# Six leading transfers reordered, and the early step order of five engines written out as a list, in a fused attention and channel-mix kernel

## The chip, the cores and the metric

The kernel runs on one core of a Trainium2 chip. The metric is the device time of one execution in microseconds; the number given for a kernel is the median of its runs. Five engines matter here, each of which executes its own instructions strictly in the order of the program: TensorE (PE, matmul; PEld is its weight load), VectorE (DVE), ScalarE (ACT), GpSimd (POOL) and SyncE (SP), which in this kernel issues every transfer between HBM and on-chip memory.

## What is computed

The reference, cut to what matters (B, H, S, D = 8, 8, 576, 64; the channel mix has d_model 512 and d_ff 1024):

```python
def _attn_ref(q, k, v):
    k_p = k.reshape(B, H, S // 8, 8, D).mean(axis=3)      # 72 pooled keys per head
    v_p = v.reshape(B, H, S // 8, 8, D).mean(axis=3)
    scores = np.matmul(q, k_p.transpose(0, 1, 3, 2)) / np.sqrt(D)
    scores = scores - np.max(scores, axis=-1, keepdims=True)
    attn = np.exp(scores)
    attn = attn / (np.sum(attn, axis=-1, keepdims=True) + 1e-09)
    return np.matmul(attn, v_p)

def _moe_ref(x, mu_k, mu_r, w_k, w_v, w_r):               # x: attention, heads joined
    x_prev = x shifted by one token, zeros in front
    xk = mu_k * x + (1.0 - mu_k) * x_prev
    xr = mu_r * x + (1.0 - mu_r) * x_prev
    k = np.maximum(xk @ w_k, 0.0)
    v = k * k @ w_v
    r = 1.0 / (1.0 + np.exp(-(xr @ w_r)))
    return r * v
```

## The kernel before, in words

The 8 x 576 = 4608 tokens are cut into 13 chunks of 128, 256 and then eleven times 384 tokens, and each chunk into tiles of 128 tokens (36 tiles). A tile goes through `softmax` (scores on PE, maxima and sums on DVE, exponentials on ACT, norming on POOL or DVE) and `transposed`/`transposed_rest`; a chunk goes through `attended` (attention times pooled values, then the token shift and mix on ACT, POOL and DVE), `hidden` (x times w_k, squared ReLU), `gate` (x times w_r, sigmoid) and `mixed` (hidden times w_v, times the gate, and the store). The first two chunks multiply whole float32 operands; the later ones use three matmuls on operands split into a high and a low part. The three weights arrive as 64-bit words and are turned into float32 by `convert` (ACT and DVE) and into the two parts by `split` (ACT, then DVE or POOL).

Every transfer has a short name in the string `LOADS` (line 48): `k0`, `k1` are the keys of the first batch entry, heads 0 to 3 and 4 to 7 (576 KB each); `v0`, `v1` its values; `r0`, `r1` the values behind the last 8 pooled keys of batch entries 0 and 1, in a packed form of 128 KB each; `c0` the constants (54 KB: the mix factors `mu`, a mask and a selection matrix `pick`); `q0`, `q1` and so on the queries of one tile (256 KB each); `wk0`, `wr0`, `wv0` and so on a 512 KB slice of a weight. SP issues them in the order of the string, one behind the other. In the profile `k0` is `stage<-in_kT`, `k1` is `early_sl<-in_kT`, `r1` is `early_sl<-in_vp`, `r0` is `packed<-in_vp`, `c0` is `given<-in_consts`, `q0` is the first `qs<-in_qT`.

The first work on them, by step name:

- `keys 0 0` adds the 8 neighbours of `k0` by matmuls with the identity on PE (line 570, two halves of four sums), and ACT copies the sums to `kbd` (line 612).
- `keys 0 1` does the same for `k1` in three steps on DVE (line 559 twice, line 601 for `kbd`).
- `last_values 1` and `last_values 0` take `r1` and `r0`: a PE sum with `pick` from `c0` (line 659), a cast on ACT (line 668), a subtraction on DVE (line 670), and a spread by the mask (line 680 on DVE for `r1`, line 675 on ACT for `r0`).
- `complements` computes 1 - mu from `c0` on DVE (line 440).
- `softmax 0` and `part 0 1 2` are the two halves of tile 0: scores on PE at line 729, the maximum on DVE at line 753.
- `warm` (line 424) and `filling` (line 434) are matmuls on zeros and on the identity whose results nobody reads: 4 and 40 of them.

The program is written by a planner, the class `Order`. Every piece of work is a generator whose steps are named after it (`keys 0 1`, `hidden 2 4`) and yield an engine and an estimated length. The planner keeps a clock of its own for each engine, and picks, step by step, among the steps that could start first, the one with the earliest due time (`add` sets it; the table `EARLIER` shifts it). The order of its picks is the order of the instructions on each engine. A buffer that a step takes is the one that came free first by the planner's clock. If the string `PLAN` holds names, the planner takes those steps, in that order, before it chooses any itself, and while names are left the extra delay `spare` of a PE step is not added:

```python
at = max(self.free[eng],
    t[4][1] if t[4][0] == eng else t[1] + (t[5] if eng == "pe" and not self.plan else 0.0))
...
if self.plan:
    name = self.plan.pop(0)
    at, t = next((at, t) for at, t in ready if t[6] == name)
else:
    first = min(at for at, _ in ready)
    ...
```

In the kernel before, `PLAN` is empty: the planner chooses all 2821 steps.

Of the kernel before, what the change touches and what calls it, by code (L numbers as in the profile page):

```python
# [45 lines left out]
REBASE = 2.0 ** -((1023 - 127) // 8)  # L46

LOADS = (
    "k0 c0 r1 k1 r0 q0 wk0 q1 q2 v0 wk1 v1 wk2 q4 wk3 k2 wk4 q3 wk5 wk6 k3 wk7 wr0 wr1 wr2 wr3 v3 "
    "wv2 wv0 wv1 wv3 q5 wv4 wv5 wv6 v2 wv7 "  # L50
)

# [55 lines left out]
}  # L108
PLAN = ""
SPARE = 0.5  # L110
SECOND = 0.0
NEXT = 14.0
# [5 lines left out]
class Order:  # L118
# [8 lines left out]
    def __init__(self):  # L127
# [8 lines left out]
        self.plan = []  # L136
        for step in PLAN.split(", ") if PLAN else ():
            name, _, times = step.partition(" x")
# [1085 lines left out]
```

## Time and profile before

| | |
|---|---|
| median of 3 runs | 631.24 us (631.03 to 631.31) |
| the profiled execution | 631.48 us, of which 629.7 us lie between its first and its last instruction (the span) |
| instructions | 9238 |
| busy, share of the span | PE 99%, PEld 87%, DVE 63%, ACT 56%, POOL 34% |
| read and written in HBM | 40.43 MB and 9.44 MB |
| granted TensorE clock | 1.000 |

The busy times are sums of the durations that the profiler recorded; a PE that is busy may still be busy with matmuls that nobody needs (`warm` and `filling`). All transfers go through one queue (q1). The profiled execution took 0.24 us longer than the median; 1.8 us of it lie around the span.

### The profile page before, as it was taken

How to read it: one execution, taken by the hardware profiler on the slowest of the kernel's cores; microseconds unless marked ns; L12 is line 12 of the kernel's file. 1: busy time of each engine (PE TensorE's matmuls, PEld its weight loads, DVE VectorE, ACT ScalarE, POOL GpSimd, SP SyncE). 2: the span in 40 equal slices, each digit the busy share in tenths (PEclk: the TensorE clock that was granted, in tenths of full speed). 3: DMA queues.
4: the chain of work that ended last, by engine and by line, in shares of the span. 5: the costliest groups of instructions: out<-in, count | busy, mean ns of one | idle time of the engine just before them, and what ended most of it. 6: DMA issues, size and time to landing. Idle time of an engine off the chain costs nothing.

```text
span 629.7 us, 9238 instructions
## 1 busy us (share of the span) xinstructions
PE 622.3 (99%) x3355; PEld 548.0 (87%) x3355; DVE 394.2 (63%) x792; ACT 350.9 (56%) x755; POOL 215.3 (34%) x338
## 2 busy tenths in 40 slices
PE   8999999999999999999999999999999999999997
PEld 8986559988989989989988988988988988988986
DVE  5999969968824645937635665759854655553411
ACT  3776866766525855556645555545655556454320
POOL 1422287448015128128125019217415106104000
PEclk9999999999999999999999999999999999999999
DMA  8696332051330012411011051032100100000001
GB/s 309 233 364 217 108 128 89 18 179 52 125 110 34 0 34 82 137 34 51 0 34 52 25 193 45 6 137 78 55 34 34 33 18 35 17 1 18 33 1 50
DMA packets 19005, 50.45 MB, mean 80 GB/s; under 512 B 2256, under 2 KB 2512, under 8 KB 18960
## 3 DMA queue, kind: packets, MB, share of 16 engines
q1 hardware_dynamic: 18960, 49.87, 22.6%
q8 instruction: 26, 0.43, 0.3%
q14 instruction: 19, 0.16, 0.1%
HBM read 40.43 MB, written 9.44 MB: 79 GB/s over the span
## 4 chain that ended last, share of the span: by engine, by line
PE 88%; ACT 3%; DVE 3%; POOL 3%; DMA 2%; issue 1%; SPq 0%; POOLq 0%; ACTq 0%; DVEq 0%
PE mm L1029 30%; PE mm L1111 29%; PE mm L1078 16%; PE bank L931 5%; PE sc L729 4%; PE bank L833 2%; DMA got_wr<-in_w_r 1%; DMA stage<-in_kT 1%; PE bank L424 1%; PE bank L434 1%; PE bank L888 1%; POOL stage L559 1%; ACT e L776 0%; ACT tmp L522 0%; DVE got_wk L527 0%
## 5 line engine op out<-in xcount | busy, mean ns | idle before, releaser
L1029 PE MATMUL mm<-xkh,w_k 128*128 128x384 f32 x704 | 180.9, 337 | 0.0
L1111 PE MATMUL mm<-w_v,sh 128*128 128x512 f32 x528 | 173.3, 394 | 0.0
L1029 PEld LDWEIGHTS mm<-xkh,w_k 128*128 128x128 f32 x704 | 126.0, 188 | 1.0 <-issue 0.6
L1029 PE MATMUL mm<-xkl,w_k 128*128 128x384 f32 x352 | 117.7, 335 | 0.0
L1111 PEld LDWEIGHTS mm<-w_v,sh 128*128 128x128 f32 x528 | 99.3, 188 | 19.4
L1111 PE MATMUL mm<-w_v,sl 128*128 128x512 f32 x264 | 103.0, 390 | 0.0
L791 POOL TENSOR_TENSOR px<-e,sm 128x64 f32<-128x64 f32 (+1 forms) x33 | 10.9, 331 | 225.7 <-DVE sm L785 219.9
L1078 PE MATMUL mm<-w_r,xrh 128*128 128x512 f32 x264 | 86.0, 397 | 0.0
L985 DVE SCALAR_TENSOR_TENSOR xm<-bank,given,t 128x384 f32<-128x384 f32 x88 | 50.6, 612 | 40.2 <-POOL t L959 23.0
L944 ACT ACTIVATE t<-bank,om_sb 128x384 f32<-128x384 f32 (+1 forms) x96 | 47.9, 573 | 50.0 <-PE bank L931 49.8
L1052 ACT CAST sh<-rk 128x384 fp32r<-128x384 f32 x88 | 45.0, 513 | 50.2 <-DVE rk L1046 50.0
L1121 DVE TENSOR_TENSOR rs<-mm,rs 128x512 f32<-128x512 f32 x36 | 24.8, 689 | 70.9 <-PE mm L1111 70.7
L1054 DVE TENSOR_TENSOR sl<-rk,sh 128x384 fp32r<-128x384 f32 x88 | 51.9, 592 | 24.8 <-ACT sh L1052 24.4
L1029 PEld LDWEIGHTS mm<-xkl,w_k 128*128 128x128 f32 x352 | 66.1, 188 | 0.0
L1046 DVE SCALAR_TENSOR_TENSOR rk<-mm,rk 128x384 f32<-128x384 f32 x88 | 48.6, 553 | 17.4 <-ACT rk L1039 17.0
L1078 PEld LDWEIGHTS mm<-w_r,xrh 128*128 128x128 f32 x264 | 49.6, 188 | 10.2
L1003 POOL TENSOR_TENSOR xkl<-xm,xkh 128x384 fp32r<-128x384 f32 x44 | 44.7, 1017 | 37.2 <-ACT xkh L1001 37.1
L1111 PEld LDWEIGHTS mm<-w_v,sl 128*128 128x128 f32 x264 | 49.7, 188 | 8.7
L559 POOL TENSOR_TENSOR stage<-stage 128x512 f32<-128x512 f32 (+7 forms) x59 | 51.3, 878 | 13.7 <-DVE w_k L552 11.4
L1039 ACT ACTIVATE rk<-mm 128x384 f32<-128x384 f32 x88 | 43.0, 489 | 20.9 <-PE mm L1029 19.9
L1078 PE MATMUL mm<-w_r,xrl 128*128 128x512 f32 x132 | 51.4, 389 | 0.0
L1003 POOL TENSOR_TENSOR xrl<-xm,xrh 128x384 fp32r<-128x384 f32 x44 | 44.8, 1019 | 1.3 <-ACT xrh L1001 1.2
(144 smaller groups left out, 972.8 us busy)
## 6 DMA issues: line engine op xcount, KB each, us to landing
qs<-in_qT SPq DMA_DIRECT2D x36, 256.0 KB, 3.5
out<-rs SPq DMA_DIRECT2D x36, 256.0 KB, 2.0
stage<-in_kT SPq DMA_DIRECT2D x15, 576.0 KB, 3.8
stage<-in_vm SPq DMA_DIRECT2D x15, 512.0 KB, 4.5
got_wk<-in_w_k SPq DMA_DIRECT2D x8, 512.0 KB, 6.8
got_wv<-in_w_v SPq DMA_DIRECT2D x8, 512.0 KB, 7.5
stage<-in_vr SPq DMA_DIRECT2D x6, 384.0 KB, 4.1
got_wr<-in_w_r SPq DMA_DIRECT2D x4, 512.0 KB, 8.0
```

The lines of the kernel that those rows point to most:

```text
L559: nc_eng.tensor_tensor(out=st[:, :, :w], in0=st[:, :, :w], in1=st[:, :, w:2 * w], op=ALU.add)
L931: nc.tensor.matmul(out=xp[:, o], lhsT=v, rhs=p, start=(q == 0), stop=(q == len(terms) - 1))
L944: nc.scalar.activation(out=ts[m][:, 1:n + 1], in_=xp, func=AF.Copy, scale=om_sb[:, m, g:g + 1])
L985: nc.vector.scalar_tensor_tensor(out=xm[:, :n], in0=bank[:, :n], scalar=mu_sb[:, m, g:g + 1], in1=ts, op0=ALU.mult, op1=ALU.add,)
L1003: nc.gpsimd.tensor_tensor(out=lo, in0=xm[:, :n], in1=hi, op=ALU.subtract)
L1029: nc.tensor.matmul(out=hp, lhsT=w[:, o], rhs=x[:, ct, :n], start=(ct == 0 and k == 0), stop=(ct == NCT - 1 and k == len(terms) - 1),)
L1039: nc.scalar.activation(out=rk[:, :n], in_=hp, func=AF.Relu)
L1046: nc.vector.scalar_tensor_tensor(out=rk[:, :n], in0=hp, scalar=0.0, in1=rk[:, :n], op0=ALU.max, op1=ALU.mult)
L1052: nc.scalar.copy(out=sh[:, :n], in_=rk[:, :n])
L1054: nc.vector.tensor_tensor(out=operand("sl", c)[:, jt, :n], in0=rk[:, :n], in1=sh[:, :n], op=ALU.subtract)
L1078: nc.tensor.matmul(out=bank, lhsT=x[:, ct, o], rhs=w, start=(ct == 0 and k == 0), stop=(ct == NCT - 1 and k == len(terms) - 1),)
L1111: nc.tensor.matmul(out=bank, lhsT=s[:, o], rhs=w, start=(jt == 0 and k == 0), stop=(jt == NJT - 1 and k == len(terms) - 1),)
```

## The change

Two strings change, and nothing else. In `LOADS` the first six names change their order, and all later ones stay where they are. `PLAN` goes from empty to a list of 691 steps: 223 on PE, 213 on DVE, 141 on ACT, 61 on POOL and 53 on SP. It runs from the first transfer into the hidden layer of chunk 2. The 53 SP steps are called `loads` and name no transfer; each issues the next one of `LOADS`.

```diff
 LOADS = (
-    "k0 c0 r1 k1 r0 q0 wk0 q1 q2 v0 wk1 v1 wk2 q4 wk3 k2 wk4 q3 wk5 wk6 k3 wk7 wr0 wr1 wr2 wr3 v3 "
+    "k0 k1 q0 c0 r1 r0 wk0 q1 q2 v0 wk1 v1 wk2 q4 wk3 k2 wk4 q3 wk5 wk6 k3 wk7 wr0 wr1 wr2 wr3 v3 "
     "wv2 wv0 wv1 wv3 q5 wv4 wv5 wv6 v2 wv7 "
 )
...
-PLAN = ""
+PLAN = (
+    "loads, constants, warm, loads, constants, warm x2, loads, constants, warm, loads, warm, constants x2, "
+    "filling, loads, filling x2, constants, loads, filling x2, constants, filling, loads, filling, keys 0 0, "
+    "complements, loads x2, last_values 1, loads, keys 0 0, last_values 1, keys 0 1, loads, last_values 0, "
+    "keys 0 0, loads, last_values 1, filling, keys 0 1, filling, loads, last_values 1, softmax 0, keys 0 1, "
+    "last_values 1, filling, part 0 1 2, softmax 0, last_values 0, convert k 0, filling, last_values 0, "
+    "loads, filling, softmax 0, softmax 1, last_values 0, part 0 1 2, loads, convert k 0, softmax 0, "
...
+    "split v 1, hidden 2 5, softmax 11, hidden 2 6, hidden 2 5, split v 3, hidden 2 6, softmax 8, "
+    "hidden 2 7, softmax 8, softmax 10, hidden 2 6, hidden 2 7 x2, split v 3, softmax 11, hidden 2 7, "
+    "softmax 11, hidden 2 2"
+)
```

More of the change, by code (lines that the diff above doesn't have):

```diff
@@ L108 @@
 }
-PLAN = ""
+PLAN = (
[3 more added lines that the diff above has]
+    "keys 0 0, loads, last_values 1, filling, keys 0 1, filling, loads, last_values 1, softmax 0, keys 0 1, "
[19 rows of a table added]
+    "filling, transposed_rest 2, filling, convert k 4, hidden 0 2, transposed_rest 2, loads, softmax 3, "
[59 rows of a table added]
+)
 SPARE = 0.5
```

73 rows, old and new, of the table PLAN are left out of this document.

## The prediction

> **What bounds the kernel now.** I read the page first (sections 1 and 4), then the idle time of PE by stretches and by releaser, and last the first 12 us engine by engine. From the page, the busy times and the chain that ended last:
>
> ```profile
> PE 622.3 (99%) x3355; PEld 548.0 (87%) x3355; DVE 394.2 (63%) x792; ACT 350.9 (56%) x755; POOL 215.3 (34%) x338
> PE 88%; ACT 3%; DVE 3%; POOL 3%; DMA 2%; issue 1%; SPq 0%; POOLq 0%; ACTq 0%; DVEq 0%
> ```
>
> PE is the bound. The next view gives the busy time of each engine by stretch (the first number is the length, the second PE's busy time); below it stands what PE waited for up to 116 us.
>
> ```profile
> 0.00:24.00 24.00, 21.97 (x159) 20.71 (x159) 15.91 (x46) 12.20 (x36) 4.81 (x17) 1.00 0.78 282
> 24.00:116.00 92.00, 90.54 (x479) 69.39 (x480) 82.00 (x178) 67.42 (x151) 44.87 (x67) 1.00 0.49 174
> 116.00:625.90 509.90, 509.80 (x2720) 457.85 (x2718) 295.62 (x569) 271.23 (x570) 165.59 (x255) 1.00 0.16 54
> ...
> PE bank L424 <- DVE tmp L420: 1.5, 1, 1.5
> PE mm L1029 <- DVE sh L1046: 0.5, 1, 0.5
> PE sc L729 <- ACT e L762: 0.5, 1, 0.5
> PE mm L1029 <- DVE xkh L985: 0.5, 1, 0.5
> PE mm L1111 <- ACT rs L1086: 0.3, 1, 0.3
> PE bank L888 <- DVE pr L870: 0.2, 1, 0.2
> ```
>
> The reader is to see how little idle time there is. PE idles 2.0 and 1.5 us in the first two stretches, 3.5 us together, and the six waits add up to the same 3.5. The first, 1.5 us before the first matmul, waits for a DVE memset that the change does not touch. So 2.0 us (0.5 + 0.5 + 0.5 + 0.3 + 0.2) is all the early idle time that any change of order could recover, and behind 116 us there is 0.1. PE's instructions do not change in number or shape, those of `warm` and `filling` included. Only waits can move the time.
>
> **The change, part by part.** *The list.* Set against the order that the planner finds in the kernel before, the list is the same, name for name, over all 691 steps and so on each of the five engines. It can be seen in the rows below: "keys 0 0, last_values 1, keys 0 0, last_values 0, filling x2, softmax 0" are PE's L570, L659, L570, L659, L434, L729. So up to the end of the list (a matmul of `hidden 2 2`, at about 116 us) no engine's order changes. What is left is (a) six transfers in another order under unchanged engines, and (b) what the planner picks after the list, since its clocks stand differently there.
>
> *(a) The transfers.* SP's issues, each transfer's time from issue to landing, and the rate in 40 slices of 0.3 us from 0 to 12 us:
>
> ```profile
> 0.74 0.37 SPq L505 DMA_DIRECT2D stage<-in_kT  x1
> 1.16 0.42 SPq L466 DMA_DIRECT2D given<-in_consts  x1
> 1.64 0.42 SPq L493 DMA_DIRECT2D early_sl<-in_vp  x1
> 2.10 0.43 SPq L505 DMA_DIRECT2D early_sl<-in_kT  x1
> 2.58 0.43 SPq L493 DMA_DIRECT2D packed<-in_vp  x1
> 3.05 0.43 SPq L473 DMA_DIRECT2D qs<-in_qT  x1
> ...
> stage<-in_kT SPq DMA_DIRECT2D x1, 576.0 KB, 3.7
> given<-in_consts SPq DMA_DIRECT2D x1, 54.0 KB, 3.5
> early_sl<-in_vp SPq DMA_DIRECT2D x1, 128.0 KB, 3.3
> early_sl<-in_kT SPq DMA_DIRECT2D x1, 576.0 KB, 6.2
> packed<-in_vp SPq DMA_DIRECT2D x1, 128.0 KB, 6.1
> qs<-in_qT SPq DMA_DIRECT2D x1, 256.0 KB, 6.2
> GB/s 0 0 0 0 0 108 61 77 246 399 415 369 381 267 318 164 154 154 169 224 208 350 410 323 370 292 311 379 423 444 369 423 403 396 423 410 423 444 423 423
> ```
>
> Issue plus landing time gives the landings of before: k0 4.4, c0 4.7, r1 4.9, k1 8.3, r0 8.7, q0 9.3 us. The six issue slots stay; k1 moves from 2.10 to 1.16, q0 from 3.05 to 1.64, c0 from 1.16 to 2.10, r1 from 1.64 to 2.58, r0 from 2.58 to 3.05. Everything from wk0 on keeps its slot and the same 1718 KB ahead of it, so I cost the later transfers at nothing. k1 and r1 also exchange the two halves of one buffer, which costs nothing.
>
> Landings after: k0 stays at 4.4. The rest I bound from both sides. Without any dip, what follows k0 moves at the 415 GB/s of the better slices: k1 (576 KB, 0.59 MB) lands 1.4 us later, at 5.8, c0 (886 KB behind k0) at 6.6, r1 (1014 KB, 1.04 MB) at 6.9. If the dip of the five slices from 4.5 to 6.0 us (154 to 224 GB/s, 865 in sum where 2000 would be five full ones) comes again, it costs (2000 - 865) / 400 x 0.3 = 0.85 us: k1 6.7, c0 7.5, r1 7.8. At worst the bytes arrive no faster than in the rows of before, the slowest engine included: there 1462 KB had landed at 8.7 (r0) and 1718 KB at 9.3 (q0), so c0 (1462 KB) lands at 8.7 and r1 (1590 KB) halfway, at 9.0. I take the middle one, r1 at 7.8, since the dip is in the only start that was measured, and keep 6.9 and 9.0 as ends.
>
> The Trainium skill, page "DMA: Bandwidth & Descriptors", section "Specifications", puts the ceiling of the 16 engines at 435 GB/s; by that figure alone r1 would land 2.4 us behind k0, at 6.8, an estimate. The trace agrees with it from 9.6 us on (396 to 444 GB/s a slice) and not between 4.5 and 6.0 us, so the rows' 7.8 stays.
>
> What do the landings move? The timelines of PE (up to the first matmul of the hidden layer), DVE and ACT:
>
> ```profile
> 7.08 1.15 PE L570 MATMUL mm<-stage,ident 128*128 128x144 f32 x8
> 8.07 0.60 PE L659 MATMUL mm<-early_sl,given 128*96 128x128 f32 x4
> 8.50 1.15 PE L570 MATMUL mm<-stage,ident 128*128 128x144 f32 x8
> 9.49 0.60 PE L659 MATMUL mm<-packed,given 128*96 128x128 f32 x4
> 9.92 0.61 PE L434 MATMUL bank<-ident 128*128 128x128 f32 x4
> 10.37 0.69 PE L729 MATMUL sc<-kbd,qs 128*128 128x144 f32 x4
> 11.11 0.66 PE L729 MATMUL sc<-kbd,qs 128*128 128x144 f32 x4
> 23.95 0.49 PE L1029 MATMUL mm<-stage,got_wk 128*128 128x128 f32 x2
> 4.66 0.17 DVE L440 TENSOR_SCALAR om_sb<-given 128x8 f32<-128x8 f32 x1 [2.11 <-DMA given<-in_consts]
> 8.32 0.76 DVE L559 TENSOR_TENSOR early_sl<-early_sl 128x576 f32<-128x576 f32 x1 [3.49 <-DMA early_sl<-in_kT]
> 9.11 0.29 DVE L670 TENSOR_TENSOR vq<-mm,vq 32x128 fp32r<-32x128 f32 x1
> 9.43 0.46 DVE L559 TENSOR_TENSOR early_sl<-early_sl 128x288 f32<-128x288 f32 x1
> 10.14 0.61 DVE L601 TENSOR_TENSOR kbd<-early_sl 64x144 f32<-64x144 f32 x2
> 11.80 0.46 DVE L753 TENSOR_REDUCE mx<-sc 128x4 f32<-128x288 f32 x1 [0.60 <-PE sc L729]
> 8.70 0.26 ACT L668 CAST vq<-mm 96x128 fp32r<-96x128 f32 x1 [6.69 <-PE mm L659]
> 9.69 0.56 ACT L612 COPY kbd<-mm 64x144 f32<-64x144 f32 x2 [0.72 <-PE mm L570]
> ```
>
> - k1 earlier: DVE waited 3.49 us for it. After, DVE waits for c0 first (`complements` stands ahead in its order): 7.5, then 0.2 for that and 0.76 for the first halving, done at 8.4 to 8.5 instead of 9.08. But its next instruction is `last_values 1` (L670), which needs ACT's cast, done at 8.70 + 0.26 = 8.96, and that hangs on PE's L659. So L670 starts at 9.0 instead of 9.11, and `kbd` (L601) ends at about 10.65 instead of 10.75. PE comes to the scores that need it (the second L729) only at 11.11, behind fillers, and DVE then waits 0.60 us for PE (L753). Worth 0.1 us on DVE and nothing on the path; the cover is PE's fixed order.
> - q0 earlier: it landed at 9.3, and PE's scores at 10.37 waited for ACT's `kbd`, done at 9.69 + 0.56 = 10.25. Worth nothing.
> - c0, r1 later: PE's first L659 at 8.07 needs both. At 7.8 they are there, with 0.27 us to spare: nothing. At 9.0 PE stands 0.9 us, with both L570 halves' end, ACT's two instructions and the whole of tile 0 queued behind; no idle time of PE behind it would take this up, since its later waits are on engines that slip with it.
> - r0 one place later: in q0's place, 9.3 at most, needed at 9.49. Worth nothing.
>
> *(b) After the list.* The planner goes on with 2821 - 691 = 2130 steps of its own. Within the list a PE step's `spare` (0.5 or 1.0) is not added and the transfers land at other times by its clock, so it may pick otherwise from here, and take other buffers. No row shows another order. The gain is bounded by the 0.1 us that PE idles there. The loss is bounded by the waits of the early part: 0.5 us each, one in each of the ten chunks left, 5 us. I take 0, by the row nearest to it: the same planner, with the same due times, already ran 509.9 us with 0.1 us idle, and its choice between steps that are ready goes by due times, which do not move.
>
> The sum: 0 (list) + 0 (transfers) + 0 (after the list) on the profiled execution's 631.48 us; the median stands 0.24 below it, so 631.2.
>
> **The rivals.**
>
> *r1 comes too late.* For it: r1 moves behind 1462 KB, and with the rate of before it lands at 9.0, 0.9 us after PE wants it. Against: c0 and r1, which stood just ahead of the dip, are now behind k1 and q0. It gives 632.1, still within 0.2%. The Trainium skill, the same page, section "Queues, rings and completion order", says that each engine consumes its descriptors in ring order; the trace agrees, with all six landings in the order of issue. By that rule r1 can't overtake k1 and q0, and nothing but their pace decides.
>
> *The planner goes astray after the list (slower).* Place: PE behind 116 us, at chunk boundaries where scores, transposes and attention are slipped between the big products. Price: 0.5 us a wait, as at L1029 and L729. It decides from three such waits on (1.5 us, 632.7), and at ten gives 636. For it: the plan's clock is shifted against that of before. Against: 0.1 us of idle time in all that the same rules ordered before.
>
> *The early keys pay after all (faster).* If the three 0.5 us waits and the two small ones all went, 2.0 us: 629.2. Three of the five must go to be seen. Against: they wait for exponentials, squares and mixes whose order is the same as before.
>
> **How the numbers follow.** A measurement of this kernel tells about 0.2% (1.26 us) from no change. Nothing moves (631.2, within 0.5): 0.60. r1 late (632.1): 0.14, "same" too. Astray after the list: 0.19, all of it slower. Early keys pay: 0.07, faster. So faster 0.07, same 0.74, slower 0.19. The range goes from 630.0, which takes in half of the faster case, to 633.2, which takes in r1 late and up to four waits of the slower one.
>
> **What would show it.** The order of all engines up to 116 us is that of before. k1 lands near 6.7 and DVE's L559 starts well ahead of 8.3, yet `kbd` (L601) still ends near 10.7. The first L659 starts at 8.07, and the L729 of tile 0 at 10.37; an L659 at 9 with a wait on `in_vp` is the first rival. The first matmul of the hidden layer (L1029, 23.95 before) comes within 0.2 us of that. PE's idle time behind 116 us tells of the second. The prediction is wrong if PE's waits add up to 1.3 us more or less than 3.5, or if the part behind 116 us gets longer in PE's own pace.

## The result: 8 us slower, all of it behind the list

| | before | after |
|---|---|---|
| median | 631.27 us (631.03 to 631.43, 4 runs) | 639.44 us (639.21 to 639.61, 4 runs) |
| ratio | | 1.013, 95% interval 1.0112 to 1.0147 |
| profiled execution, span | 631.48, 629.7 us | 639.4, 637.6 us |

In the profile of the changed kernel, line 1 of the page and the chain that ended last:

```profile
PE 623.7 (98%) x3355; PEld 547.6 (86%) x3355; DVE 394.5 (62%) x792; ACT 351.2 (55%) x755; POOL 215.4 (34%) x338
PE 86%; DVE 6%; ACT 3%; POOL 2%; DMA 1%; issue 1%; SPq 0%; DVEq 0%; ACTq 0%; POOLq 0%
```

The same 3355 matmuls are in it. Span less busy time is PE's idle time: 637.6 - 623.7 = 13.9 us, against 629.7 - 622.3 = 7.4 before. So 6.5 of the 7.9 us by which the span grew are new idle time, and 1.4 are longer busy time of the same matmuls. Some of that is the waits over again: in the records matmuls overlap (337 ns each at the hidden layer, one every 187 ns behind 116 us in the kernel before, 2720 in 509.80 us), and ahead of a wait the last one runs on alone, which counts as busy. By an estimate from these two figures that is 0.1 to 0.15 us a wait, about 1 us in all. Where the idle time lies, by stretches (length, then the busy time of PE, PEld, DVE, ACT and POOL), the changed kernel first:

```profile
0.00:24.00 24.00, 21.84 (x163) 20.74 (x164) 16.42 (x47) 12.23 (x36) 5.36 (x19) 1.00 0.80 291
24.00:116.00 92.00, 90.47 (x476) 68.70 (x474) 81.86 (x177) 67.84 (x150) 44.64 (x65) 1.00 0.48 172
116.00:200.00 84.00, 77.61 (x399) 67.13 (x400) 50.74 (x106) 40.98 (x85) 26.52 (x37) 1.00 0.29 94
200.00:400.00 200.00, 200.00 (x1086) 180.66 (x1085) 116.85 (x229) 114.91 (x245) 76.53 (x123) 1.00 0.16 55
400.00:634.00 234.00, 233.75 (x1237) 210.32 (x1235) 128.07 (x236) 115.20 (x240) 62.37 (x96) 1.00 0.10 37
```

The kernel before has no gap in the third stretch:

```profile
116.00:200.00 84.00, 84.00 (x442) 74.31 (x441) 54.42 (x115) 45.26 (x94) 30.84 (x45) 1.00 0.29 97
```

The first two rows are those of before to within 0.2 us, and behind 200 us PE is full again. The loss sits in 116 to 200 us, where 6.4 us are idle and 43 fewer matmuls fit (399 against 442). PE's timeline there, those rows that begin with a wait (in brackets, with what ended it):

```profile
117.68 0.30 PE L972 MATMUL bank<-ident,pr 128*128 128x128 f32 x1 [1.79 <-DVE pr L954]
151.55 0.33 PE L972 MATMUL bank<-ident,pr 128*128 128x128 f32 x1 [1.47 <-DVE ptl L930]
152.14 0.33 PE L972 MATMUL bank<-ident,pr 128*128 128x128 f32 x1 [0.27 <-DVE ptl L930]
153.13 0.63 PE L917 MATMUL bank<-ident,pm 128*128 128x128 f32 x4 [0.66 <-POOL t L1039]
155.84 0.62 PE L1113 MATMUL mm<-xkh,w_k 128*128 128x384 f32 x2 [0.92 <-ACT xkh L1085]
156.92 0.45 PE L1113 MATMUL mm<-xkl,w_k 128*128 128x384 f32 x1 [0.46 <-POOL xkl L1087]
171.06 0.62 PE L1113 MATMUL mm<-xkh,w_k 128*128 128x384 f32 x2 [0.93 <-DVE rk L1130]
```

Seven waits, 6.5 us together. They stand in two places. **Place 1** is the row at 117.68: PE comes to a transpose of tile 8 (`transposed_rest 8`, line 972) before DVE has made `pr`, its input. DVE was not idle: between the two instructions that make `pr` (116.47 and 117.32) it halved keys (line 643, 0.75 us). The row is the very first matmul that stands elsewhere in PE's order than before, directly behind the last listed one, which ends at 115.9 us. **Place 2** is the other six, 151 to 171 us, at the start of chunk 3: the transposes of tiles 9 to 11 are bunched, and the mixing of chunk 3 (`attended 3 0`) now stands behind `mixed 2 2`, the last big products of chunk 2 that could have covered it. So the hidden layer (line 1113) waits for `xkh`, `xkl` and `rk`.

**What leads the planner astray** can be read in `run` (printed above). The variable `eng` says on whose clock a step's length is booked. When the planner chooses for itself, it sets `eng`. When it takes a name from `PLAN`, it does not: `eng` still holds the engine of whichever thread the loop over `ready` looked at last. So 691 lengths go to wrong clocks. Following the planner's arithmetic, its clocks after step 691 stand like this:

| planner's clock, us | PE | DVE | ACT | POOL | SP |
|---|---|---|---|---|---|
| before, own choice | 110.5 | 110.6 | 108.7 | 110.2 | 98.1 |
| after, from the list | 101.5 | 99.3 | 91.8 | 91.0 | 54.2 |

To the planner ACT is then free 10 us ahead of PE and POOL as well, where before they stood within 2 us. It believes that inputs are ready which are not. Of the picks that follow it makes 50 of 1061 PE places other than before, 84 of DVE's 761, 34 of ACT's, 23 of POOL's and 3 of SP's.

### The profile page after: what moved, and what is told of

Read it like the earlier page. It is cut to its first block, busy times and chain, and to the rows that moved or that the text cites. A ratio compares the mean times of both kernels' runs of the same rounds, so it can differ in the third digit from the quotient of the medians.

```text
span 637.6 us, 9236 instructions
## 1 busy us (share of the span) xinstructions
PE 623.7 (98%) x3355; PEld 547.6 (86%) x3355; DVE 394.5 (62%) x792; ACT 351.2 (55%) x755; POOL 215.4 (34%) x338
## 4 chain that ended last, share of the span: by engine, by line
PE 86%; DVE 6%; ACT 3%; POOL 2%; DMA 1%; issue 1%; SPq 0%; DVEq 0%; ACTq 0%; POOLq 0%
PE mm L1195 31%; PE mm L1113 27%; PE mm L1162 14%; PE bank L1015 5%; PE sc L813 4%; PE bank L917 2%; DMA got_wr<-in_w_r 1%; POOL stage L643 1%; DVE sl L1138 1%; PE bank L518 1%; PE mm L654 1%; DVE mx L837 1%; PE bank L508 1%; PE bank L972 0%; DVE e L854 0%
## 5 line engine op out<-in xcount | busy, mean ns | idle before, releaser
L1136 ACT CAST sh<-rk 128x384 fp32r<-128x384 f32 x88 | 45.1, 514 | 54.2 <-DVE rk L1130 53.9
```

Source lines behind the costliest of these rows:

```text
L1136: nc.scalar.copy(out=sh[:, :n], in_=rk[:, :n])
```

## The experiments

All listed times have a kernel before of their own beside them, on the same chip; the ratios are to that, and need not be the quotient of the two medians.

**1. Each half alone.** e1 keeps the list and takes the transfers back; e2 keeps the transfers and empties the list.

```diff
 e1
-    "k0 k1 q0 c0 r1 r0 wk0 ...
+    "k0 c0 r1 k1 r0 q0 wk0 ...
 e2
-PLAN = ( "loads, constants, warm, ... hidden 2 2" )
+PLAN = ""
```

> The list of 691 steps with the transfers in the old order. Theory L (the list): while the planner follows the list, it books the length of each step on the clock of whichever engine it looked at last, so its clocks are wrong where the list ends (PE 101.5, DVE 99.3, ACT 91.8, POOL 91.0 where its own planning had 110.5, 110.6, 108.7, 110.2), and it picks another order from there. The order of all engines is then that of the changed kernel, and the time 639.4 to 640.1. Theory T (the transfers): the new landing times upset the planner or the chip; with the old order of transfers the loss goes: 631.2.

> The new order of transfers with no list: the planner picks all 2821 steps itself, with 261 of 1061 PE places other than before. Theory L: no loss behind 116 us, 630.2 to 632.2. Theory T: 638 to 640.

e1: 639.37 us, ratio 1.0124 (1.0106 to 1.0142): the whole loss. Its order of instructions is that of the changed kernel on every engine but SP, and the first wait is there again:

```profile
117.49 0.30 PE L972 MATMUL bank<-ident,pr 128*128 128x128 f32 x1 [1.78 <-DVE pr L954]
```

e2 was a miss: 646.64 us, ratio 1.0232 (1.0202 to 1.0263), where 630 to 632 was expected. Without the list the planner takes the new landing times into its clocks and orders the first 116 us afresh, 261 PE places other than before, and badly. Its second stretch by engines, and then PE's timeline at the two largest waits in it:

```profile
24.00:116.00 92.00, 82.69 (x402) 59.77 (x401) 75.11 (x163) 58.78 (x137) 38.68 (x64) 0.96 0.46 164
```

```profile
40.80 3.13 PE L1029 MATMUL mm<-xkh,got_wk 128*128 128x256 f32 x8 [2.08 <-DVE xkh L985]
54.64 1.46 PE L1029 MATMUL mm<-stage,got_wk 128*128 128x128 f32 x8 [3.65 <-DVE got_wk L527]
```

So the list does two things: it keeps the start from being re-planned under the new transfers, and it upsets what is planned behind it.

**2. Which line of the planner.** There are two differences between a listed and a chosen step: the clock that is booked, and the `spare` that a listed PE step does not get. e3 mends both, e4 only the spare, e5 only the clock.

```diff
 e3 and e5
             at, t = next((at, t) for at, t in ready if t[6] == name)
+            eng = t[2][0]
 e3 and e4
-    ... t[1] + (t[5] if eng == "pe" and not self.plan else 0.0)
+    ... t[1] + (t[5] if eng == "pe" else 0.0)
```

> The changed kernel, but in the list each step is booked on its own engine, and the extra delay of PE steps is kept. All 2821 steps then come in the order of before, so only the transfers differ. Theory L: 630.6 to 631.3, PE idle behind 116 us 0.1 again. Theory T: 638 to 640.

> The changed kernel, but the extra delay of PE steps (spare) is kept while the list is followed; the booking on a wrong engine stays. Theory L: still 638 to 640. Theory S (the missing delay is what shifts the planner's clocks): 631.

> The changed kernel with one line: in the list each step is booked on its own engine; the extra delay of PE steps stays off. 2 of 1061 PE places and 20 of 761 DVE places differ from before. Theory L: 630.6 to 632. If the delay matters beside the booking: 634 or more.

| | us | ratio, 95% |
|---|---|---|
| e3, clock and spare | 631.66 | 1.0003 (0.9994 to 1.0013) |
| e4, spare alone | 641.96 | 1.0158 (1.0134 to 1.0181) |
| e5, clock alone | 631.37 | 1.0003 (0.9994 to 1.0013) |

The one line `eng = t[2][0]` takes the whole loss away, and the spare none of it. e4 came out above the 638 to 640 that was expected: its order is a little further from that of before than the changed kernel's (54 PE places against 50, by the planner's arithmetic), PE waits 2.85 us at place 1, and its profile has 10.2 us at half the granted clock behind the two places (last section). e5's stretch is full again:

```profile
116.00:200.00 84.00, 84.00 (x442) 74.23 (x441) 54.03 (x115) 45.38 (x94) 30.75 (x46) 1.00 0.29 97
```

In e3 the order of every engine but SP is that of the kernel before, so it also measures the transfers by themselves: nothing.

**3. How much each place costs.** Here, and in i1, i3 and i5 below, all steps are listed and e3's two lines are in. x1 has place 1 as before and place 2 as after, x2 the other way round.

```diff
-PLAN = ( ... 691 steps )
+PLAN = ( ... 2821 steps; x1: place 1 as before, place 2 as after; x2: place 1 as after, place 2 as before )
```

> The order behind the list differs from before in two places: PE 223 to 231 (transposed_rest 8 goes ahead of the rest of hidden 2 2, PE waited 1.8 us for DVE) and PE 249 to 304 (attended 3 0 goes behind mixed 2 2, the transposes of tiles 9 to 11 are bunched, PE waited 1.7 + 0.9 + 0.9 + 0.7 + 0.5 us). Here all 2821 steps are listed, each booked on its own engine: the first place as before, the second as in the changed kernel. If the two places are independent: 631.3 + 4.7 to 6.5, 636 to 638. If the second loss is only the echo of the first: 631 to 632.

> The other half: the first place as in the changed kernel, the second as before. Independent: 631.3 + 1.8 to 2.5, 633 to 634. If the first place drags the later ones along: 638 or more.

x2: 632.27 us, ratio 1.0019 (1.0009 to 1.0029), so place 1, with its wait of 1.8 us, costs 1.1 us (0.6 to 1.8 by the interval), less than the 1.8 to 2.5 that was expected. x1: 641.35 us, ratio 1.0163 (1.0144 to 1.0182): more than both places together, and above the 636 to 638 that was expected. It has the waits of place 2 once more, and one that is its own, from joining two orders: a query is issued at 131.3 us where the changed kernel issues it at 126.0.

```profile
134.94 1.36 PE L1087 MATMUL sc<-kbd,qs 128*64 128x144 f32 x16 [2.34 <-DMA qs<-in_qT]
```

```profile
136.00:138.00 2.00, 2.00 (x8) 1.76 (x6) 0.00 (x0) 0.02 (x1) 0.00 (x0) 0.50 0.15 54
```

The second is a row by stretches: two us at half the granted clock (0.50, the number behind the five engines) right after that wait. The wait of 2.3 us and about 1.7 us of half speed are not place 2's. Taking them off leaves about 637 for place 2, some 6 us; the whole loss less place 1 would give 7. Both are worked out, not measured. Place 2 is the main loss, and place 1 does not bring it about: with place 1 as after and the rest as before (x2), no other wait comes behind it.

**4. Where the list ends.** The changed kernel with its list cut at 600 steps, and with the first 1000 steps of before; the clocks are booked as wrongly as in the changed kernel.

```diff
-PLAN = ( ... 691 steps )
+PLAN = ( ... the first 600 )          (l6)
+PLAN = ( ... the first 1000 of before )  (l10)
```

> The changed kernel with its list cut after 600 of the 691 steps, and nothing else. The planner takes over about 15 us earlier. Theory 'booking on the wrong engine': the clocks are wrong at the end of any such list, so time is lost right behind step 600 (from about 100 us on), though at other places: 80 places of TensorE's order differ from the kernel before, against 50 with the whole list. So slower than before by 3 to 12 us, 634 to 643, with no loss ahead of 95 us. Rival 'what the list itself holds near its end makes the loss': a shorter list leaves that part to the planner, so 631 to 632.

> The changed kernel with its list made longer, the first 1000 steps of the kernel before, and nothing else; the clocks are booked as wrongly as in the changed kernel. Theory: where the list ends decides whether the planner is led astray: behind step 1000 the planner happens to pick the order of the kernel before in all places of TensorE, so 630.8 to 632, the loss gone without mending the clocks. Rival 'wrong clocks cost wherever the list ends': 634 or more, with waits behind about 165 us.

l6: 640.15 us, ratio 1.0137 (1.0123 to 1.0151); the first wait moves with the end of the list, now to 102.6 us, and the others stand again at the start of chunk 3. Two of the five:

```profile
102.62 1.25 PE L804 MATMUL sc<-kbd,qs 128*128 128x144 f32 x8 [1.71 <-DVE e L845]
152.99 0.48 PE L963 MATMUL bank<-ident,pr 128*128 128x128 f32 x1 [2.23 <-DVE pr L945]
```

l10: 631.45 us, ratio 1.0001 (0.9991 to 1.0011), with no PE wait behind 116 us. After step 1000 the same wrong clocks happen to lead to the order of before, by the planner's arithmetic on every engine. So what is lost is not a price of wrong clocks as such; it depends on the choices that are open where the list ends. The planner's order for other lengths, which was worked out but not run on the chip, shows no trend: 50 PE places differ for 691 steps, 5 for 450, 190 for 200.

**5. Can the early keys be used at all?** The first half of the scores of tile 0 needs `q0` and what `keys 0 0` makes from `k0`; the second half needs the part of `kbd` that `keys 0 1` makes from `k1`. i1 was a first try, with the whole program listed: `keys 0 0` right behind the warm-up, `last_values 1` held back until `gate 1 1` is done, `r1` loaded late for it (behind `q5`, into the buffer of `r0`), 11 fillers left out.

```diff
-    "k0 k1 q0 c0 r1 r0 wk0 q1 ...
+    "k0 k1 q0 c0 r0 wk0 q1 ... q5 r1 wv4 ...
-FILLERS = 40
+FILLERS = 29
+    packed[1] = packed[0]
+        if b == 1:
+            yield need(("gated", 1, 1))
-PLAN = ( ... warm, constants x2, filling, loads, ... keys 0 0, complements, ... last_values 1, ...
+PLAN = ( ... warm, constants x2, loads, ... keys 0 0, loads x3, keys 0 0, filling x2, keys 0 1, ...
```

> All steps listed and booked rightly, and an order that uses the early keys: keys 0 0 straight after warm on PE, keys 0 1 ahead of last_values on DVE, last_values 1 only behind gate 1 1 (r1 loaded late), 11 of 40 fillers left out. If the early keys pay once the order lets them: tile 0's scores near 8 us instead of 10, 628.3 to 630.3. If weights and DVE hold the start anyway: 631 to 632. Slower, if the TensorE clock comes up late or falls back for want of fillers: 632 to 635.

i1: 636.99 us, ratio 1.0089 (1.0062 to 1.0115), slower than any of the three cases expected. The first scores came at 7.7 us (9.8 in the changed kernel), and were paid for, as PE's timeline and two rows by stretches show:

```profile
13.93 1.32 PE L927 MATMUL mm<-early_sl,ident 128*128 128x128 f32 x8 [2.95 <-DVE e L1129]
82.53 0.36 PE L1290 MATMUL bank<-ptr,vbd_r 96*128 96x192 f32 x1 [2.53 <-DVE vbd_r L1039]
```

```profile
14.80:18.20 3.40, 3.40 (x17) 3.40 (x16) 1.67 (x6) 0.68 (x1) 0.03 (x1) 0.50 1.03 416
83.10:86.50 3.40, 3.40 (x10) 2.07 (x9) 1.73 (x4) 3.03 (x7) 2.11 (x6) 0.50 0.19 64
```

Two waits, each with 3.4 us at clock 0.50 behind it. i3 takes from this what worked and undoes what waited: `last_values 1` stays early, right behind the keys; the due time of `values 0 0`, which in i1 waited 2.95 us until DVE was done with its PSUM buffer (the row at 13.93), is moved ahead so that it takes one that is free; nine fillers are left out, and the first of those kept stand behind the scores.

```diff
-FILLERS = 40
+FILLERS = 31
-    "values 0 0": 252.4,
+    "values 0 0": -100.0,
-PLAN = ( ... filling, keys 0 0, complements, ... last_values 1, loads, keys 0 0, last_values 1, keys 0 1, ...
+PLAN = ( ... keys 0 0, loads x3, keys 0 0, last_values 1, keys 0 1, ... softmax 0, filling, ... complements, ...
```

> Builds on the version with the clock mended (631.4): the transfers in the new order, keys 0 0 multiplied right behind the warm-up, last_values 0 held back behind fillers, keys 0 1 first on VectorE, the value product of chunk 0 using the right bank of the pair. It tells whether the keys that land at 6.0 us can be turned into time at all. Theory 'the arrival of the first keys sets the start': the scores of tile 0 come about 2 us earlier, and some 1 to 2 us of it stay, 629 to 630.5. Rival 'the start is held by the chain behind the scores and by other work in the first 20 us': no gain, 631 to 632. Rival 'the moved work leaves TensorE waiting 2 us or more and the clock falls back', as in the first try of this kind: 634 to 637, with a stretch of 3.4 us at half the granted clock in the profile.

i3: 629.35 us (628.75 to 630.13, 5 runs), ratio 0.9967 (0.9954 to 0.998): the fastest version, 0.33% under the kernel before. Then i5, the same program with the old transfers:

```diff
-    "k0 k1 q0 c0 r1 r0 wk0 ...
+    "k0 c0 r1 k1 r0 q0 wk0 ...
```

> The version that uses the early keys (629.35), with the transfers put back into the order of the kernel before, and nothing else: every engine's order stays. It tells whether the gain of that version comes from the new transfer order or from the nine fillers that were left out and the moved steps alone. By the landings of before, the second half of the keys comes at 8.3 us instead of 6.0. Theory 'the gain needs the early keys': VectorE's halving, and kbd behind it, start 2.2 us later, TensorE waits about 2 us in the first 12 us, which nothing gives back: 631 to 632.5, and 633 to 634 if the clock falls back in that wait. Rival 'the fillers and the moved steps are the gain': the wait is under 0.5 us and the time stays at 629 to 630.

i5: 630.84 us (629.67 to 631.69, 12 runs), ratio 0.9992 (0.9982 to 1.0002). That is just under the 631 to 632.5 of the first theory, and above the rival's 629 to 630. The two timelines, PE and DVE, i3 and then i5:

```profile
7.93 0.73 PE L1086 MATMUL sc<-kbd,qs 128*128 128x144 f32 x4
8.72 0.66 PE L1086 MATMUL sc<-kbd,qs 128*128 128x144 f32 x4
6.05 1.25 DVE L916 TENSOR_TENSOR early_sl<-early_sl 128x576 f32<-128x576 f32 x2 [3.50 <-DMA early_sl<-in_kT]
```

```profile
9.16 0.73 PE L1086 MATMUL sc<-kbd,qs 128*128 128x144 f32 x4 [1.44 <-DMA qs<-in_qT]
10.04 0.76 PE L1086 MATMUL sc<-kbd,qs 128*128 128x144 f32 x4
8.09 1.25 DVE L916 TENSOR_TENSOR early_sl<-early_sl 128x576 f32<-128x576 f32 x2 [5.54 <-DMA early_sl<-in_kT]
```

With the old transfers PE waits 1.44 us for `q0`, and DVE starts on `k1` 2.0 us later. In medians the new transfers are worth about 1.5 us here (629.35 against 630.84; by the ratios 0.25%, with some 0.16% either way from the two intervals). Whether it is `k1` or `q0` that is worth it was not tried; the wait that PE shows is on `q0`. The fewer fillers and moved steps alone give i5's ratio, whose interval takes in no change.

## Why the prediction was wrong, step by step

The prediction said 631.2 us, 0.74 for no change; the measured 639.44 lies 6 us outside its range. One step failed, and the bound put on it; those ahead of it held.

- *The list keeps every engine's order to 116 us.* Right. PE's waits up to there are those of before, and one of 0.2 us more (3.7 us in all against 3.5):

```profile
PE bank L508 <- DVE tmp L504: 1.5, 1, 1.5
PE mm L1113 <- DVE sh L1130: 0.5, 1, 0.5
PE sc L813 <- ACT e L846: 0.5, 1, 0.5
PE mm L1113 <- DVE xkh L1069: 0.4, 1, 0.4
PE mm L1195 <- ACT rs L1170: 0.3, 1, 0.3
PE bank L1015 <- ACT whole_ptr L969: 0.2, 1, 0.2
PE bank L972 <- DVE pr L954: 0.2, 1, 0.2
```

- *(a) The transfers.* Worth nothing under this order, as said, and e3 confirms it. The landings were earlier than the middle value that I chose. SP's issues, the time from issue to landing, and the rate in slices of 0.3 us up to 12 us, in the changed kernel:

```profile
1.17 0.42 SPq L589 DMA_DIRECT2D early_sl<-in_kT  x1
2.11 0.54 SPq L550 DMA_DIRECT2D given<-in_consts  x1
2.69 0.45 SPq L577 DMA_DIRECT2D early_sl<-in_vp  x1
```

```profile
early_sl<-in_kT SPq DMA_DIRECT2D x1, 576.0 KB, 4.8
early_sl<-in_vp SPq DMA_DIRECT2D x1, 128.0 KB, 4.6
given<-in_consts SPq DMA_DIRECT2D x1, 54.0 KB, 4.8
GB/s 0 0 0 0 0 77 92 184 108 353 399 384 476 353 445 445 384 393 364 362 362 376 335 273 287 382 389 396 376 410 376 410 457 423 355 273 314 382 369 423
```

`k1` lands at 1.17 + 4.8 = 6.0 us, `c0` at 6.9, `r1` at 7.3. The dip that I carried over from before did not come again once the rate was up: from 2.7 us on no slice is under 273 GB/s. The no-dip ends (5.8, 6.6, 6.9) were nearer, or as near. (The dip was also read a slice too short: 208 GB/s from 6.0 to 6.3 us belongs to it, which makes it 1.0 us instead of 0.85.) `k1`, `c0` and `r1` land in the order of issue. The Trainium skill, page "DMA: Bandwidth & Descriptors", section "Queues, rings and completion order", says that descriptors are consumed in that order, but that a later one may finish its write before an earlier one; none did here. The same page's 435 GB/s (section "Specifications") would have put `r1` at 6.8, an estimate; measured is 7.3.

- *`kbd` hangs on PE's order, not on the keys.* Right. The step that gates DVE is the one that was named: the subtraction of `last_values 1` behind ACT's cast, and DVE then waits for PE's scores.

```profile
8.39 0.29 DVE L754 TENSOR_TENSOR vq<-mm,vq 32x128 fp32r<-32x128 f32 x1 [0.60 <-ACT vq L752]
9.43 0.61 DVE L685 TENSOR_TENSOR kbd<-early_sl 64x144 f32<-64x144 f32 x2
11.20 0.46 DVE L837 TENSOR_REDUCE mx<-sc 128x4 f32<-128x288 f32 x1 [0.71 <-PE sc L813]
```

All of this is 0.6 us earlier than forecast, but so is PE itself (its first matmul of the hidden layer starts at 23.35 instead of 23.95), and not because of the keys (last section).

- *"(b) After the list ... I take 0."* This is the step that failed: what was put at 0 was 8 us. Two parts of its reasoning were wrong. First, "its choice between steps that are ready goes by due times, which do not move": `run` first takes the earliest possible start over all clocks, which settles the engine, and asks for due times only among that engine's steps within 0.1 us of it. The clocks decide, and I had not followed how a listed step is booked on them, though the code was in front of me. Second, the row that I took as nearest, 0.1 us idle in 509.9, belongs to a planner whose clocks fit the chip. It was no evidence about the same planner with others.
- *The bound of the loss*, 0.5 us a wait and 5 us in all, was mis-sized as well. It took waits from a good order, where an input comes just too late. In a bad order PE stands until DVE or ACT has gone through what it had put ahead: 1.8 and 1.5 us in the longest cases, and 6.5 us in 54 us, not one wait in each chunk. To it come the 1.4 us of longer busy time, which no single row shows; what the estimate above leaves of them stays open.
- *The rivals.* "The planner goes astray after the list", at 0.19, is what happened, at the place that it named (transposes and attention at chunk boundaries) and beyond its price of 636 for ten waits. "r1 comes too late" did not: the first L743 started without a wait at 7.46. But `r1` had landed only 0.2 us before, and in i3 PE waits 0.2 us for it, so that was close. "The early keys pay after all" did not happen either: in the changed kernel they pay nothing, and where they pay (i3) it is because PE's order was changed to ask for them, not because the five small waits went.
- *What would show it.* "PE's idle time behind 116 us tells of the second" was the right place to look.

## What to carry to other kernels

When a hand-written order is followed by an automatic one, ask what state the automatic part starts from, and follow it through the code: a list that repeats its own choices word for word still changed what came behind it, by 8 us. Data that arrive earlier are worth something only if the engine that is the bound is ordered to ask for them earlier: the same six transfers gave nothing under the old order and about 1.5 us under a new one. A bound for a bad order must come from how much work another engine can have put ahead of the input that is missing, not from the waits of a good order.

## What the runs showed of the hardware

**TensorE's clock comes up at another moment in each profile.** The same 14 fillers behind the same warm-up, in the kernel before, in the changed one and in e5:

```profile
5.02 2.22 PE L434 MATMUL bank<-ident 128*128 128x128 f32 x14
```

```profile
4.92 1.73 PE L518 MATMUL bank<-ident 128*128 128x128 f32 x14
```

```profile
5.03 2.50 PE L519 MATMUL bank<-ident 128*128 128x128 f32 x14
```

A filler starts every 214 ns at half rate and every 111 ns at full rate. (The granted clock in the rows by stretches reads 1.00 here all the same.) From the point where the spacing changes, full rate began at 6.1, 4.8 and 6.6 us, and over all profiles between 4.5 and 7.6 us, 3 to 6 us behind the first matmul at 1.45. This is what put the changed kernel 0.6 us ahead at 7 us. A shift of that size in the first 10 us, in one profile, says nothing about a transfer.

**Every wait of PE of 2.08 us or more came with half clock here, and no single one of up to 1.79 us did.** Six of the fourteen kernels have stretches at granted clock 0.50 in the middle of their profile, 3.4 us long or twice that, and each begins within 1 us of the end of a wait. They stand at waits of 2.08 and 3.65 us (e2), 2.34 (x1), 2.53 and 2.95 (i1), 2.85 (e4) and 2.23 us (l6, among shorter ones). Of the waits behind the warm-up that stand alone, none follows those of 1.79 (the changed kernel), 1.78 (e1), 1.77 (x2) and 1.71 us (l6). The group of 1.5, 0.3 and 0.7 us at place 2 goes either way: half clock follows it in e1 and e4 and not in the changed kernel and x1. This is one profile of each kernel; it does not fix a threshold. The Trainium skill, page "TensorE: Matmul & The Clock Gate", Part 1, has the gate fall back after an idle window of about 3.4 us. The slow stretches are that long, but all of these waits but one were shorter, so by these runs a wait of 2.1 us is already at risk. A stretch of 3.4 us does 1.7 us less work than one at full speed, but that need not all be lost: e1, with one at place 2, took as long as the changed kernel without (639.37 and 639.44), and its waits for `xkh` and `xkl` behind it were 0.15 us together instead of 0.92 and 0.46.

**The transfers run slowly at the very start, and a second time only in the old order.** In the changed kernel the slow slices are the first four (77 to 184 GB/s, from 1.5 to 2.7 us), and from there until `k1` has landed the rate is 353 GB/s or more. With `c0` and `r1` in second and third place there is a second dip between 4.5 and 6.0 us, in all three profiles: down to 154 (before), 142 (e1) and 123 GB/s (i5). In the eleven with `k1` and `q0` there, no slice from 3.0 to 6.0 us is under 330. `k1` gained 2.3 us of landing time by it (8.3 to 6.0). Whether it is the small transfers or their place that makes the second dip was not tried.
